# Windowed attention and a gated MLP in one kernel: another order of the opening, and the last score groups in quarters of the array

## The chip, the core and the metric

The kernel runs on one core of a Trainium2 chip. A core has a tensor engine (PE in the profile, with its weight loads as PEld), a vector engine (DVE), a scalar engine (ACT), a general engine (POOL), a queue engine that mostly issues transfers (SP), and 16 DMA engines. Each engine works off its own list of instructions in order and waits on semaphores for the others. The metric is the device time of one execution in microseconds (us); lower is better.

## What is computed

Two blocks follow each other, for a batch of 4, 8 heads, 768 positions, head width 64:

```python
scores = scale * q @ k.T                       # per batch and head
keep   = (pos_k < 4) | ((pos_q - pos_k >= 0) & (pos_q - pos_k < 128))
a      = softmax(where(keep, scores, -1e9))
x      = (a @ v), the 8 heads side by side     # 4 x 768 x 512
h      = gelu_tanh(x @ w_in)                   # 4 x 768 x 1024
u, g   = h[..., :512], h[..., 512:]
g      = layer_norm(g) * g_ln
g      = w_sg @ g + b_sg                       # over the 768 positions
out    = x + (u * g) @ w_out
```

So each query sees four sink positions and the 128 positions up to its own.

## The kernel before

**Pairs.** Two heads make a pair, numbered `n` = 0 to 15; four pairs are one batch element. For a pair, `load` brings k, q and v from memory, 384 KB each (SP's queue; the first q goes through ACT's). k and q come in rows of 1,536 bytes, v in rows of 256 bytes. The pool `loads` holds three of each kind, so the k of pair 3 can start only when the k of pair 0 has been cast. `cast` turns them to bf16, on POOL but for the first two, which go to DVE. `columns` turns k or q by six 128x128 transposes on PE into a PSUM bank (`kps`, `qps`), and one copy by ACT or DVE puts the result into `kT` or `qT` in another element order.

**Scores.** A pair's six blocks of 128 keys are taken in three groups, `g` = 0, 1, 2, of two blocks j each. `score(n, g)` multiplies each block's keys (64 rows of the array per head, so the two heads stand in the upper and lower half) with the 256 queries that can see them (128 for the last block), into a two-bank tile `sc`; there are two such tiles (`ps_s`). In group 2 the free places take the scores of the first 32 keys for the last four query blocks, by eight matmuls that each use 64 rows and 32 columns of the array (line 273). ACT then takes the exponential of the whole tile (line 277).

**The mask.** Positions outside the band are removed in one of two ways. Where `darkened(n, g)` is true, `begin_scores` first writes a large negative number to them by two matmuls of the identity with `off` or `off0` (line 247), and the scores are accumulated on top. Else `keep_band` clears them after the exponential: on DVE by one multiplication with a 0/1 mask (line 286) or on POOL by two selects (lines 294, 296).

**Values.** `values(n, c)` does half of a pair, c = 0 or 1: 10 or 12 small matmuls of probabilities with v and two with the sinks' v (`vsink`), a reciprocal and a multiplication on DVE (lines 328, 329). `turn_x` transposes a pair's result by six PE transposes and one copy. The PSUM pool `ps_m` has four banks, for all of `kps`, `qps`, `av`, `xps` and the MLP's tiles.

**The MLP.** With a batch element's four `xT` there, `open_v` and `hidden` run x @ w_in (tiles `hv`, `hu`), the norm, and later `spatial` (`vs`, line 423) and `project` (`o_ps`, line 454); these fill the time of the next four pairs' attention.

**Order.** The schedule is written out by hand (`manual_schedule`): every engine does its instructions in the order in which the code emits them. Lines 596 to 678 are the opening, the stretch in question: four pairs of attention with nothing to fill the gaps, and the first loads. Before it PE runs 16 small matmuls on the identity (`WARM`) and, after the first transposes, `keep_busy(3)`. SP's queue takes k, q of pair 1, v of pair 0, k, q of pair 2, k of pair 3, four small copies that spread the sinks (`spread_sinks`), q of pair 3, v of pairs 1, 2, 3, and then `hold_loads(0)`, a tiny transfer that waits for the first half of w_in. POOL issues the weight transfers between its casts. `vsink` is cleared in two parts, 13 of 16 pairs' worth by DVE and the rest by POOL (`NZ`).

Of the kernel before, what the change touches and what calls it, by code (L numbers as in the profile page):

```python
# [18 lines left out]
def kernel(  # L19
# [14 lines left out]
    nc = tc.nc  # L34
    V, G, A = nc.vector, nc.gpsimd, nc.scalar
# [7 lines left out]
    NT = S // 128  # L43
    HP = H // 2
    KD = DM // 128
    KU = DF // 128
    NP = B * HP
    HT = NT // 2
# [19 lines left out]
    iden = consts.tile([128, 128], BF16, name="iden")  # L68
# [21 lines left out]
    def load(n, which, eng=None, in_rows=False):  # L90
        b, hp = divmod(n, HP)
        src = dict(k=k, q=q, v=v)[which]
        dst = loads.tile([128, 2, NT, 64], F32, name=which + "_sb")
        order = "h (t p) d -> p h t d" if which == "v" or in_rows else "h (p t) d -> p h t d"
        (eng or nc.sync).dma_start(  # L95
            out=dst, in_=src[b, 2 * hp:2 * hp + 2].rearrange(order, t=NT))
        raw[n, which] = dst
# [3 lines left out]
    def cast(n, which, eng):  # L101
        src = raw.pop((n, which))
        if which == "v":
            eng.tensor_copy(v_bufs[n % NV][:, :, :, 0:64], src)  # L104
            return
        dst = work.tile([128, NT, 128], BF16, name=which + "_bf")
        eng.tensor_copy(dst.rearrange("p t (h d) -> p h t d", h=2), src)  # L107
        flat[n, which] = dst
# [15 lines left out]
    load(0, "k")  # L124
    load(0, "q", A)
    A.dma_start(out=g_rows, in_=moe_g_ln.rearrange("(c p) -> c p", p=128))
    for n, which in ((1, "k"), (1, "q"), (0, "v"), (2, "k"), (2, "q")):
        load(n, which)
    NZ = 13


    DARK = -2.0 ** 33
# [25 lines left out]
    G.memset(off0[0:n_sink, 0:256], 0.0)  # L158
    G.memset(vsink_flat[:, NZ * 520:].bitcast(F32), 0.0)
    V.memset(vsink_flat[:, 0:NZ * 520], 0.0)  # L160
    iden4 = consts.tile([KU, KU], F32, name="iden4")
    V.tensor_copy(iden4, iden[0:KU, 0:KU])

    def band_mask(m, dark):
        V.tensor_scalar(out=m, in0=dark, scalar1=-1.0 / DARK, scalar2=1.0,
                        op0=ALU.mult, op1=ALU.add)

    def spread_sinks(i):

        pairs = slice(0, HP) if i == 0 else slice(HP, NP)  # L170
        for a in range(4):
            nc.sync.dma_start(out=vsink[32 * a:32 * a + n_sink, a, pairs], in_=vst[i])
# [8 lines left out]
    def load_w_in(cols, cs=slice(0, KD)):  # L181
        G.dma_start(out=w_in_sb[:, cs, cols],
                    in_=moe_w_in.rearrange("(c p) f -> p c f", p=128)[:, cs, cols])
# [25 lines left out]
    def bank(shape, dtype, name):  # L209
        return ps_m.tile(shape, dtype, name=name, tag="m")  # L210
# [1 line left out]
    kTs, qTs, exps, avs = {}, {}, {}, {}  # L212
    x_sb, xT = {}, {}

    def columns(n, which, eng):
        src = flat.pop((n, which))
        ps = bank([128, NT, 128], BF16, which + "ps")
        for t in range(NT):
            nc.tensor.transpose(ps[:, t, :], src[:, t, :], iden)  # L219
        dst = work.tile([128, S], BF16, name=which + "T")  # L220
        o, i = dst.rearrange("c (p t) -> c p t", t=NT), ps.rearrange("c t p -> c p t")
        if eng is A:
            A.copy(o, i)
        else:
            eng.tensor_copy(o, i)  # L225
        (kTs if which == "k" else qTs)[n] = dst

    def columns_by_dma(n):
# [6 lines left out]

    def darkened(n, g):

        return (n, g) in ((0, 1), (0, 2), (1, 2), (2, 1), (2, 2), (3, 0), (3, 1), (3, 2), (HP, 0))

    scores = {}  # L240

    def begin_scores(n, g):
        sc = scores[n, g] = ps_s.tile([128, 1024], F32, name="sc", tag="s")
        if darkened(n, g):
            used = 512 if g < HT - 1 else 384
            for l in range(2):
                nc.tensor.matmul(sc[:, 512 * l:512 * l + used], iden,  # L247
                                 (off0 if g == 0 else off)[:, 0:used],
                                 start=True, stop=False)

    def score(n, *groups):
        kT, qT = kTs[n], qTs[n]
        if 0 in groups:
            exps[n] = work.tile([128, HT, 1024], BF16, name="ex", bufs=3)
        for g in groups:
            if (n, g) not in scores:
                begin_scores(n, g)
            sc = scores.pop((n, g))
            w, dark = 0, darkened(n, g)
            for j in (2 * g, 2 * g + 1):  # L260
                n_q = min(256, S - 128 * j)
                for l in range(2):
                    rows = slice(64 * l, 64 * l + 64)
                    nc.tensor.matmul(sc[:, 512 * l + w:512 * l + w + n_q],  # L264
                                     kT[rows, 128 * j:128 * (j + 1)],
                                     qT[rows, 128 * j:128 * j + n_q], start=not dark,
                                     stop=not dark or j % 2 == 1)
                w += n_q
            if g == HT - 1:
                for a in range(4):  # L270
                    for l in range(2):
                        rows = slice(64 * l, 64 * l + 64)
                        nc.tensor.matmul(
                            sc[32 * a:32 * (a + 1), 512 * l + w:512 * (l + 1)], kT[rows, 0:32],
                            qT[rows, 128 * (a + 2):128 * (a + 3)], start=True, stop=True,
                            tile_position=(64 * l, 32 * a))
            A.activation(out=exps[n][:, g, :], in_=sc, func=AF.Exp, scale=scale)  # L277

    def keep_band(n, g, eng):
        if darkened(n, g):  # L280
            return
        ex = exps[n][:, g, :].rearrange("p (l c) -> p l c", l=2)
        w = 512 if g < HT - 1 else 384
        if eng is V:
            m = mask0 if g == 0 else mask
            V.tensor_mul(ex[:, :, 0:w], ex[:, :, 0:w],  # L286
                         m[:, 0:w].unsqueeze(1).to_broadcast([128, 2, w]))
            return
        half = ex[:, :, 0:512].rearrange("p l (j s c) -> p l j s c", j=2, s=2)
        diag, prev = half[:, :, :, 0, :], half[:, :, :, 1, :]  # L290
        if g == HT - 1:
            prev = prev[:, :, 0:1, :]
        nj = prev.shape[2]
        eng.affine_select(out=diag, in_=diag, compare_op=ALU.is_ge, fill=0.0, base=0,  # L294
                          pattern=[[0, 2], [0, 2], [1, 128]], channel_multiplier=-1)
        eng.affine_select(out=prev, in_=prev, compare_op=ALU.is_ge, fill=0.0, base=-1,
                          pattern=[[0, 2], [0, nj], [-1, 128]], channel_multiplier=1)
# [35 lines left out]
    def turn_x(n, eng):  # L333
        b, hp = divmod(n, HP)
        ps = bank([128, NT, 128], BF16, "xps")
        for t in range(NT):
            nc.tensor.transpose(ps[:, t, :], x_sb[b][:, hp, t, :], iden)  # L337
        if eng is A:
            A.copy(xT[b][:, hp, :], ps.rearrange("p t c -> p (t c)"))
        else:  # L340
            eng.tensor_copy(xT[b][:, hp, :], ps.rearrange("p t c -> p (t c)"))
# [248 lines left out]
    def keep_busy(count):  # L590

        ps = bank([128, 512], F32, "idle")
        for i in range(count):
            nc.tensor.matmul(ps, iden, off, start=True, stop=True)

    cast(0, "k", V)
    cast(0, "q", V)
    band_mask(mask, off)
    begin_scores(0, 1)
    columns(0, "k", A)  # L600
    columns(0, "q", V)
    band_mask(mask0, off0)
    keep_busy(3)
    cast(1, "k", G)
    cast(1, "q", G)
    load(3, "k")
    spread_sinks(0)
    load(3, "q")
    load(1, "v")
    load(2, "v")  # L610
    load(3, "v")


    score(0, 0, 1)
    columns(1, "k", V)
    columns(1, "q", V)
    cast(0, "v", G)
    keep_band(0, 0, V)
    cast(2, "k", G)
    cast(2, "q", G)  # L620
    score(0, 2)
    score(1, 0, 1)
    columns(2, "k", A)
    columns(2, "q", V)
    keep_band(1, 0, V)
    cast(3, "k", G)
    cast(3, "q", G)
    score(1, 2)
    for cs in (slice(0, 2), slice(2, KD)):
        load_w_in(slice(DF, d_ff), cs)  # L630
    cast(1, "v", G)
    keep_band(1, 1, G)
    values(0, 0)
    values(0, 1)
    score(2, 0)
    columns(3, "k", A)
    score(2, 1)
    columns(3, "q", V)
    keep_band(2, 0, V)
    cast(2, "v", G)  # L640
    score(2, 2)
    turn_x(0, V)
    values(1, 0)
    score(3, 0)
    values(1, 1)
    score(3, 1)
    values(2, 0)
    score(3, 2)
    cast(3, "v", G)
    load_w_in(slice(0, DF))  # L650
    load_sinks(1)
    load_w_sg()
    values(2, 1)
    turn_x(1, A)

    hold_loads(0, w_in_sb[0:1, 0, DF:DF + 16].bitcast(F32))
# [145 lines left out]
```

## Time and profile before

| | |
|---|---|
| median of 3 runs | 167.34 us (166.82 to 167.85) |
| profiled execution, its own time | 167.47 us |
| its span in the trace | 165.8 us |
| mean granted PE clock | 0.995 |
| PE busy | 154.7 us, 93% of the span |
| DVE, ACT, POOL busy | 132.0, 110.2, 78.0 us |
| DMA | 31.09 MB, 188 GB/s over the span |
| start of the first `hv` matmul, where the opening ends | 24.43 us |
| the chain of work that ended last | PE 80%, DVE 7%, DMA 4% |

The span is 1.7 us shorter than the device time of the same execution; that rest lies around the program's own instructions. The timeline merges neighbouring instructions of one line into a row: start, length, engine, line, operation, output and inputs, shape, count, and in brackets the idle time before the row and what ended it. Matmul lengths contain a modelled run-out of some 0.17 us that overlaps the next one, so the pace of PE is read from start to start.

### The profile page before, as it was taken

To read this page: it belongs to the slowest core of one execution; us is meant where nothing else is said; L and a number is where in the kernel's file an instruction comes from. 1 tells how busy PE (TensorE), PEld (TensorE's weight loads), DVE (VectorE), ACT (ScalarE), POOL (GpSimd) and SP (SyncE) were. 2 spreads that over 40 slices of the span, in tenths; PEclk is the share of its full clock that TensorE was granted. 3 is DMA by queue.
4 is the path that set the end of the run, shared out by engine and by line. 5 is a ranking of instruction groups with operands and counts; after the bars stand their busy time and mean duration, and the time that the engine had idled before them with its cause. 6 is when DMAs were issued, how large, how long until landed. Compare 5 with 4: busy or idle time off the path is not lost.

```text
span 165.8 us, 4053 instructions
## 1 busy us (share of the span) xinstructions
PE 154.7 (93%) x1558; PEld 91.0 (55%) x1558; DVE 132.0 (80%) x316; ACT 110.2 (66%) x150; POOL 78.0 (47%) x115
## 2 busy tenths in 40 slices
PE   3878999999999999999999999999999999999950
PEld 3545574566567665565666645554565645555430
DVE  6776984996899986799889994999999959997520
ACT  3188878879977689598887475679749357511220
POOL 6469771105899979500279997000996000000000
PEclk9999999999999999999999999999999999999997
DMA  4999979999999979999912999899932310040352
GB/s 135 332 324 266 211 91 287 211 305 310 293 228 313 254 250 333 304 213 218 192 66 51 115 239 216 182 237 218 209 65 47 129 65 0 0 183 18 123 198 73
DMA packets 60194, 31.09 MB, mean 188 GB/s; under 512 B 48356, under 2 KB 57080, under 8 KB 60168
## 3 DMA queue, kind: packets, MB, share of 16 engines
q1 hardware_dynamic: 56800, 27.47, 69.4%
q0 software_dynamic: 2944, 2.77, 10.4%
q10 hardware_dynamic: 424, 0.53, 1.0%
q8 instruction: 14, 0.23, 0.6%
q14 instruction: 12, 0.10, 0.2%
HBM read 24.81 MB, written 6.29 MB: 188 GB/s over the span
## 4 chain that ended last, share of the span: by engine, by line
PE 80%; DVE 7%; DMA 4%; SPq 3%; issue 1%; ACT 1%; POOL 1%; POOLq 0%; ACTq 0%
PE vs L423 16%; PE hu L380 13%; PE o_ps L454 11%; PE hv L361 9%; PE av L320 7%; PE sc L264 6%; DMA q_sb<-in_q_dram 4%; PE hv L368 4%; SPq L95 3%; PE xps L337 2%; PE av L326 2%; PE qps L219 2%; PE kps L219 2%; PE o_ps L460 2%; PE sc L247 2%; DVE gv L426 1%
## 5 line engine op out<-in xcount | busy, mean ns | idle before, releaser
L277 ACT ACTIVATE ex<-sc 128x1024 bf16<-128x1024 f32 x48 | 47.5, 1024 | 12.5 <-PE sc L264 9.1
L423 PE MATMUL vs<-wsgT,vn 128*128 128x384 bf16 x192 | 35.3, 326 | 0.1
L294 POOL TENSOR_SCALAR_AFFINE_SELECT ex<-ex 128x512 bf16<-128x512 bf16 x25 | 17.0, 680 | 30.8 <-issue 15.2
L423 PEld LDWEIGHTS <-vn 128*128 128x128 bf16 x192 | 17.7, 97 | 10.5 <-DVE vn L413 0.2
L454 PE MATMUL o_ps<-w_out_sb,gT 128*128 128x512 bf16 x92 | 23.3, 380 | 0.1
L380 PE MATMUL hu<-xT,w_in_sb 128*128 128x384 bf16 x128 | 22.1, 326 | 0.0
L426 DVE SCALAR_TENSOR_TENSOR gv<-vs,g_sb,b_bc 128x384 bf16<-128x384 f32 x32 | 19.5, 611 | 2.7 <-PE vs L423 2.3
L372 DVE BATCH_NORM_STATS2 st<-v_all 128x6 f32<-128x512 f32 x24 | 16.1, 671 | 4.5 <-ACT v_all L370 4.5
L370 ACT ACTIVATE v_all<-hv 128x512 f32<-128x512 f32 x24 | 13.3, 599 | 8.6 <-PE hv L368 8.2
L107 POOL CAST k_bf<-k_sb 128x768 bf16<-128x768 f32 x15 | 12.6, 841 | 13.3 <-DMA k_sb<-in_k_dram 13.2
L361 PE MATMUL hv<-w_in_sb,xT 128*128 128x512 bf16 x72 | 18.8, 379 | 0.0
L329 DVE TENSOR_TENSOR x<-av,rcps 128x384 bf16<-128x384 f32 x32 | 17.8, 557 | 1.1
L429 DVE TENSOR_TENSOR gT<-gv,uT 128x384 bf16<-128x384 bf16 x32 | 17.0, 532 | 1.9
L383 ACT ACTIVATE uT<-hu 128x384 bf16<-128x384 f32 x32 | 15.7, 492 | 4.1 <-PE hu L380 3.7
L463 ACT COPY o_sb<-o_ps 128x512 f32<-128x512 f32 x13 | 7.4, 593 | 14.7 <-PE o_ps L460 13.1
L264 PE MATMUL sc<-qT,kT 64*128 64x256 bf16 x192 | 15.7, 264 | 1.3 <-DVE qT L225 1.1
L380 PEld LDWEIGHTS <-w_in_sb 128*128 128x128 bf16 x128 | 12.3, 98 | 8.0
L320 PE MATMUL av<-v_sb,ex 128*128 128x65 bf16 x352 | 16.1, 195 | 0.0
L104 POOL CAST v_sb<-v_sb 128x768 bf16<-128x768 f32 x16 | 14.6, 912 | 2.4 <-DMA v_sb<-in_v_dram 2.4
L320 PEld LDWEIGHTS <-ex 128*128 128x128 bf16 x352 | 13.0, 98 | 4.2 <-issue 1.1
L107 POOL CAST q_bf<-q_sb 128x768 bf16<-128x768 f32 x15 | 14.1, 940 | 2.4 <-DMA q_sb<-in_q_dram 2.2
L286 DVE TENSOR_TENSOR ex<-ex,mask 128x1024 bf16<-128x1024 bf16 x14 | 13.1, 933 | 2.3 <-ACT ex L277 2.1
(90 smaller groups left out, 219.9 us busy)
## 6 DMA issues: line engine op xcount, KB each, us to landing
k_sb<-in_k_dram SPq DMA_DIRECT2D x16, 384.0 KB, 6.2
v_sb<-in_v_dram SPq DMA_DIRECT2D x16, 384.0 KB, 6.4
out_dram<-o_sb SPq DMA_DIRECT2D x23, 256.0 KB, 2.8
q_sb<-in_q_dram SPq DMA_DIRECT2D x15, 384.0 KB, 6.1
wsg_sb<-in_moe_w_sg_dram POOLq DMA_DIRECT2D x2, 576.0 KB, 11.1
w_in_sb<-in_moe_w_in_dram POOLq DMA_DIRECT2D x2, 256.0 KB, 6.3
w_in_sb<-in_moe_w_in_dram POOLq DMA_DIRECT2D x1, 512.0 KB, 5.5
w_out_sb<-in_moe_w_out_dram POOLq DMA_DIRECT2D x1, 512.0 KB, 8.3
```

The lines of the kernel that those rows point to most:

```text
L107: eng.tensor_copy(dst.rearrange("p t (h d) -> p h t d", h=2), src)
L264: nc.tensor.matmul(sc[:, 512 * l + w:512 * l + w + n_q], kT[rows, 128 * j:128 * (j + 1)], qT[rows, 128 * j:128 * j + n_q], start=not dark, ...
L277: A.activation(out=exps[n][:, g, :], in_=sc, func=AF.Exp, scale=scale)
L294: eng.affine_select(out=diag, in_=diag, compare_op=ALU.is_ge, fill=0.0, base=0, pattern=[[0, 2], [0, 2], [1, 128]], channel_multiplier=-1)
L320: nc.tensor.matmul(av[:, m, l, :], probs(j, l, half), v_sb[:, l, j, :], start=first, stop=False)
L329: V.tensor_mul(x_sb[b][:, hp, HT * c:HT * (c + 1), :].rearrange("p i (l d) -> p i l d", l=2), av[:, :, :, 0:64], rcp.to_broadcast([128, HT ...
L361: nc.tensor.matmul(hvs[b, j], xT[b][:, c, 128 * j:128 * (j + 1)], w_in_sb[:, c, DF:], start=(c == 0), stop=False)
L380: nc.tensor.matmul(h_ps[:, 0:NH], w_in_sb[:, c, 128 * f:128 * (f + 1)], xT[b][:, c, NH * n:NH * (n + 1)], start=(c == 0), stop=(c == KD - 1))
L423: nc.tensor.matmul(vs[:, 0:NH], vns[b][:, si, 128 * f:128 * (f + 1)], wsgT[:, si, cols], start=(si == 0), stop=(si == NT - 1))
L426: V.scalar_tensor_tensor(out=gv, in0=vs[:, 0:NH], scalar=g_sb[:, f:f + 1], in1=b_bc[:, cols], op0=ALU.mult, op1=ALU.add)
L429: V.tensor_mul(gTs[b][:, f, cols], gv, uTs[b][:, f, cols])
L454: nc.tensor.matmul(o_ps, gTs[b][:, c, rows], w_out_sb[:, c, :], start=(c == 0), stop=(c == KU - 1 and not by_act))
```

## The change

It does six things. (1) k and q of all four opening pairs are queued ahead of any v; the sinks' copies follow v of pair 1. (2) `columns` can copy in parts, and the k and q of pair 0 and the q of pair 1 are copied in two halves. (3) Pairs 0 and 1 are wholly masked on PE (groups (0,0), (1,0), (1,1) added), and (2,1) and (3,0) are masked by DVE instead; POOL's selects of (1,1) go. (4) The emission order of the opening is new: the scores and copies of pairs 0 to 2 come before the first `values`, and the k copies of pairs 2 and 3 move from ACT to DVE. (5) DVE clears 10 pairs' worth of `vsink` and POOL 6; the copy to `iden4` comes later; `keep_busy` does 2. (6) In group 2 of every pair the two blocks' scores are made by 16 matmuls of 64 rows and 32 columns in place of 4 of 64 rows and 128 columns.

```diff
--- before.py
+++ after.py
@@ -124,9 +124,10 @@
     load(0, "k")
     load(0, "q", A)
     A.dma_start(out=g_rows, in_=moe_g_ln.rearrange("(c p) -> c p", p=128))
-    for n, which in ((1, "k"), (1, "q"), (0, "v"), (2, "k"), (2, "q")):
-        load(n, which)
-    NZ = 13
+    for n in (1, 2):
+        load(n, "k")
+        load(n, "q")
+    NZ = 10
 
 
     DARK = -2.0 ** 33
@@ -159,7 +160,6 @@
     G.memset(vsink_flat[:, NZ * 520:].bitcast(F32), 0.0)
     V.memset(vsink_flat[:, 0:NZ * 520], 0.0)
     iden4 = consts.tile([KU, KU], F32, name="iden4")
-    V.tensor_copy(iden4, iden[0:KU, 0:KU])
 
     def band_mask(m, dark):
         V.tensor_scalar(out=m, in0=dark, scalar1=-1.0 / DARK, scalar2=1.0,
@@ -212,17 +212,20 @@
     kTs, qTs, exps, avs = {}, {}, {}, {}
     x_sb, xT = {}, {}
 
-    def columns(n, which, eng):
+    def columns(n, which, eng, parts=1):
         src = flat.pop((n, which))
         ps = bank([128, NT, 128], BF16, which + "ps")
         for t in range(NT):
             nc.tensor.transpose(ps[:, t, :], src[:, t, :], iden)
         dst = work.tile([128, S], BF16, name=which + "T")
-        o, i = dst.rearrange("c (p t) -> c p t", t=NT), ps.rearrange("c t p -> c p t")
-        if eng is A:
-            A.copy(o, i)
-        else:
-            eng.tensor_copy(o, i)
+        for h in range(parts):
+            p = slice(128 // parts * h, 128 // parts * (h + 1))
+            o = dst.rearrange("c (p t) -> c p t", t=NT)[:, p, :]
+            i = ps.rearrange("c t p -> c p t")[:, p, :]
+            if eng is A:
+                A.copy(o, i)
+            else:
+                eng.tensor_copy(o, i)
         (kTs if which == "k" else qTs)[n] = dst
 
     def columns_by_dma(n):
@@ -235,7 +238,7 @@
 
     def darkened(n, g):
 
-        return (n, g) in ((0, 1), (0, 2), (1, 2), (2, 1), (2, 2), (3, 0), (3, 1), (3, 2), (HP, 0))
+        return n < 2 or (n, g) in ((2, 2), (3, 1), (3, 2), (HP, 0))
 
     scores = {}
 
@@ -259,12 +262,16 @@
             w, dark = 0, darkened(n, g)
             for j in (2 * g, 2 * g + 1):
                 n_q = min(256, S - 128 * j)
-                for l in range(2):
-                    rows = slice(64 * l, 64 * l + 64)
-                    nc.tensor.matmul(sc[:, 512 * l + w:512 * l + w + n_q],
-                                     kT[rows, 128 * j:128 * (j + 1)],
-                                     qT[rows, 128 * j:128 * j + n_q], start=not dark,
-                                     stop=not dark or j % 2 == 1)
+                for a in range(4 if g == HT - 1 else 1):
+
+                    wide = 32 if g == HT - 1 else 128
+                    for l in range(2):
+                        rows, part = slice(64 * l, 64 * l + 64), slice(wide * a, wide * (a + 1))
+                        nc.tensor.matmul(sc[part, 512 * l + w:512 * l + w + n_q],
+                                         kT[rows, 128 * j + wide * a:128 * j + wide * (a + 1)],
+                                         qT[rows, 128 * j:128 * j + n_q], start=not dark,
+                                         stop=not dark or j % 2 == 1,
+                                         **(dict(tile_position=(64 * l, 32 * a)) if wide == 32 else {}))
                 w += n_q
             if g == HT - 1:
                 for a in range(4):
@@ -596,61 +603,63 @@
     cast(0, "k", V)
     cast(0, "q", V)
     band_mask(mask, off)
+    begin_scores(0, 0)
     begin_scores(0, 1)
-    columns(0, "k", A)
-    columns(0, "q", V)
+    columns(0, "k", A, 2)
+    columns(0, "q", V, 2)
     band_mask(mask0, off0)
-    keep_busy(3)
+    V.tensor_copy(iden4, iden[0:KU, 0:KU])
+    keep_busy(2)
     cast(1, "k", G)
     cast(1, "q", G)
     load(3, "k")
+    load(3, "q")
+    for n in range(2):
+        load(n, "v")
     spread_sinks(0)
-    load(3, "q")
-    load(1, "v")
-    load(2, "v")
-    load(3, "v")
+    for n in range(2, HP):
+        load(n, "v")
 
 
     score(0, 0, 1)
     columns(1, "k", V)
-    columns(1, "q", V)
-    cast(0, "v", G)
-    keep_band(0, 0, V)
     cast(2, "k", G)
     cast(2, "q", G)
     score(0, 2)
-    score(1, 0, 1)
-    columns(2, "k", A)
-    columns(2, "q", V)
-    keep_band(1, 0, V)
+    columns(1, "q", V, 2)
     cast(3, "k", G)
     cast(3, "q", G)
+    score(1, 0, 1)
+    columns(2, "k", V)
+    columns(2, "q", V)
     score(1, 2)
+    score(2, 0)
+    columns(3, "k", V)
+    columns(3, "q", V)
+    score(2, 1)
+    cast(0, "v", G)
     for cs in (slice(0, 2), slice(2, KD)):
         load_w_in(slice(DF, d_ff), cs)
     cast(1, "v", G)
-    keep_band(1, 1, G)
+    keep_band(2, 0, V)
+    score(2, 2)
     values(0, 0)
     values(0, 1)
-    score(2, 0)
-    columns(3, "k", A)
-    score(2, 1)
-    columns(3, "q", V)
-    keep_band(2, 0, V)
+    score(3, 0)
+    keep_band(2, 1, V)
+    turn_x(0, V)
     cast(2, "v", G)
-    score(2, 2)
-    turn_x(0, V)
     values(1, 0)
-    score(3, 0)
+    score(3, 1)
     values(1, 1)
-    score(3, 1)
+    keep_band(3, 0, V)
+    score(3, 2)
     values(2, 0)
-    score(3, 2)
+    values(2, 1)
     cast(3, "v", G)
     load_w_in(slice(0, DF))
     load_sinks(1)
     load_w_sg()
-    values(2, 1)
     turn_x(1, A)
 
     hold_loads(0, w_in_sb[0:1, 0, DF:DF + 16].bitcast(F32))
```

## Prediction

> **What bounds the kernel now.** I read the page first: the engines' busy shares, the strip over time, and the shares of the chain that ended last.
>
> ```profile
> PE 154.7 (93%) x1558; PEld 91.0 (55%) x1558; DVE 132.0 (80%) x316; ACT 110.2 (66%) x150; POOL 78.0 (47%) x115
> ...
> PE   3878999999999999999999999999999999999950
> ...
> PE 80%; DVE 7%; DMA 4%; SPq 3%; issue 1%; ACT 1%; POOL 1%; POOLq 0%; ACTq 0%
> ```
>
> PE is full from the fourth slice (12 us) to the end, so what counts is when PE's list gets through. The busy share hides pace, so next comes PE's timeline, read from start to start.
>
> ```profile
> 8.21 0.61 PE L264 MATMUL sc<-qT,kT 64*128 64x256 bf16 x8 [0.38 <-DVE qT L225]
> 8.75 0.51 PE L219 MATMUL kps<-iden,k_bf 128*128 128x128 bf16 x6
> ...
> 10.13 0.34 PE L264 MATMUL sc<-qT,kT 64*128 64x256 bf16 x4
> 10.40 0.25 PE L273 MATMUL sc<-qT,kT 64*32 64x128 bf16 x8
> 11.18 0.39 PE L264 MATMUL sc<-qT,kT 64*128 64x256 bf16 x4 [0.53 <-DVE qT L225]
> 11.79 0.40 PE L264 MATMUL sc<-qT,kT 64*128 64x256 bf16 x4 [0.22 <-ACT ex L277]
> ...
> 13.08 0.51 PE L219 MATMUL qps<-iden,q_bf 128*128 128x128 bf16 x6 [0.45 <-POOL q_bf L107]
> ...
> 14.12 0.25 PE L273 MATMUL sc<-qT,kT 64*32 64x128 bf16 x8
> 14.30 0.48 PE L320 MATMUL av<-v_sb,ex 128*128 128x65 bf16 x10
> ...
> 24.43 1.47 PE L361 MATMUL hv<-w_in_sb,xT 128*128 128x512 bf16 x6
> ```
>
> From the first score (8.21) to the first `hv` (24.43) the view names 1.2 us of idle PE (0.53, 0.22, 0.45). The opening is nearly all PE work. DVE's timeline shows its own load there:
>
> ```profile
> 7.20 0.96 DVE L225 COPY qT<-qps 128x768 bf16<-128x768 bf16 x1 [0.89 <-PE qps L219]
> ...
> 15.54 0.18 DVE L328 RECIPROCAL rcps<-av 128x6 f32<-128x6 f32 x1
> ...
> 16.23 0.18 DVE L328 RECIPROCAL rcps<-av 128x6 f32<-128x6 f32 x1
> ...
> 18.25 1.53 DVE L286 TENSOR_TENSOR ex<-ex,mask 128x1024 bf16<-128x1024 bf16 x1
> ```
>
> A copy of 768 elements takes 0.96 us, half a pair's values 0.69 (15.54 to 16.23), a mask multiplication 0.69 to 1.53 (the group's shortest and longest).
>
> **The quarters (part 6).** Four score matmuls of 256 columns take 0.33 us when the array's shape changes after them (15.31 to 15.64 in the same view), eight take 0.54 (8.21 to 8.75): four cost 0.21, the change of shape about 0.12. The eight quarter matmuls of line 273 take 0.18 (14.12 to 14.30). Less one change, 0.06 is left, the time of one 128-column stream (six transposes take 0.35), so eight ran side by side. A group 2 now takes 0.27 + 0.18 = 0.45. New: all 24 matmuls have one shape, so one change falls away: streams of 256, 128 and 128 columns, 0.107 + 0.053 + 0.053, start spacing 0.03, one change 0.12, together 0.31 to 0.36. I take 0.36: 0.09 saved per group, 1.4 us over 16, if PE sets the end everywhere. Lower end nothing. Four groups lie in the opening; the other twelve give at most 1.08. DVE is nearly as full as PE there:
>
> ```profile
> 50.00:60.00 10.00, 10.00 (x150) 6.84 (x149) 9.68 (x20) 7.67 (x9) 9.29 (x14) 1.00 0.99 256
> ```
>
> (third number in us: PE, then PEld, DVE 9.68, ACT, POOL). So I count 0.9 of the 1.08.
>
> **The start (parts 2, 3, 5).** The masks of (0,0) are two more 512-column matmuls ahead of the first transposes. At that time two take 1.06 us, 0.43 each without the run-out. PE ends masks at 4.50 + 4 x 0.43 = 6.2 instead of 5.4; the k was ready at 5.70, so the transposes start 0.55 later. Halves win it back: the first score needs only half of qT, 0.54 us instead of 0.96 (384 elements cost 0.56 in line 329's row; bounds 0.48 and 0.56). First score at 8.2: nothing gained. The shorter clearing on DVE (2.88 to 2.2 us) is hidden, since the first cast waits for its k until 5.08; POOL's longer one ends near 5.9, and its next k comes at 6.48; without that cover it would cost 0.7. `iden4` (0.24) falls where DVE waits for pair 1's k; one `keep_busy` less shortens a wait only.
>
> **The loads (part 1).** POOL's casts show the landings: q or k follow each other by 1.06 to 1.1 us, a v takes 1.75. Without v, k2, q2, k3, q3 land at about 9.2, 10.2, 11.3, 12.4 and v of pair 0 at 14.1. On SP, v of pair 3 now waits for the cast of pair 0's v (to 14.9, before 10.6); behind it stand `hold_loads` and pair 4's loads, which waited for w_in until 21.07 anyway. POOL issues w_in after that cast, at 15 as now. v of pair 3 lands near 20.5; its matmuls come at 24. All hidden; uncovered, a late v 3 would cost up to 1 us.
>
> **The new order (part 4), the term that decides.** Exponentials go at 0.98 us each, and there are two `sc` tiles. (0,2) can start at 9.7 as now. Its group ends at 10.5, q of pair 1 is transposed to 11.0, its first half copied to 11.55: score (1,0) at 11.6 (now 11.18). Masks (0.52) and scores (0.33) of (1,0), (1,1) bring PE to 12.75. Then pair 2 is transposed, and DVE copies k and q one after the other, 13.3 to 15.1 (now ACT takes k beside it). PE has finished (1,2) at 14.1 and waits for q until 15.15: 1.0 us. Pair 3 is transposed from 15.5, DVE copies until 17.85. Only now DVE comes to the work that it had begun at 11 before: mask (2,0), values (0,0), (0,1). With 1.2 us for the mask (between 0.69 and 1.53; POOL casts beside it, as beside the 1.53) pair 0 is done at 17.85 + 1.2 + 2 x 0.69 = 20.4. PE arrives at `turn_x(0)` at 18.7 and waits 1.7 us. After that PE needs: rest of the transposes 0.17, values 0.38 + 0.54 + 0.38 + 0.54 + 0.41 + 0.54, score (3,1) 0.85, (3,2) 0.78, two `turn_x` 0.66: 5.25, to 25.7. DVE needs: masks 1.2 and 0.9 (the last with less of POOL beside it), xT 0.47, four values 2.76: 25.7, then `turn_x(2)` 0.33: 26.0. I take 25.8 for the first `hv`: 1.4 later than 24.43 (the four quarter groups are in it).
>
> Bounds: masks at 0.69 give 25.2 (+0.75); at 1.53 DVE reaches 27.05, `hv` 27.4 (+2.9). If PE waits no more than now, only its work counts: -0.4. Masks moved between pairs are even on PE in the sum (two groups of 0.52 added after 8.2, two taken away).
>
> **Sum.** 167.47 (this execution; span 165.8 and 1.67 around it) + 1.4 - 0.9 = 167.97. The median is 0.13 lower: 167.8.
>
> **Rivals.**
> (A) The opening flows as now: DVE's late backlog is bridged, and PE waits 1.2 us as before. For it: k and q come 1 to 2 us earlier, and DVE's work is nearly the same in sum. Against: two copies in a row stand before score (2,0), and three masks and eight values after 17.85. Then -0.4 - 1.08: 165.9; with 0.4 from the halves 165.5. 0.20.
> (B) Slower: PE can't feed 24 pairs of weight load and matmul in 0.36 us. Eight go at once (10.40), but in the values each pair costs 30 ns (12 from 14.68 to 15.05), a row that the array's own 65 columns explain. If the pairs of group 2 go at 30 ns, a group takes 0.72 + 0.12, 0.39 more than now, and this decides in all 16: +6 in all, 174. It decides from about 15 ns a pair (0.45 a group). 0.07.
> The Trainium skill, "TensorE: Matmul & The Clock Gate", section "Wait — 56ns, not 53.3ns?", speaks for (B): matmuls start no closer than about 25 ns apart, however few columns they have. By that a group would last 0.6 us and the sum be about 4 us higher; the eight of line 273 in 0.18 us disagree with it for a burst of eight, and no run here shows one of 24.
> (C) Slower: the masks on DVE last 1.53 us each, beside POOL's casts and weight issues: +2.9 - 0.9, 169.3. 0.12.
> (D) The quarters shorten PE but DVE or ACT set the pace later: +1.4, 168.7. 0.06.
>
> **Chances and range.** The forecast, an opening 0.7 to 2.2 later and quarters worth 0.5 to 1.1, holds 0.55, all within 1% (1.7 us, about what a measurement of this kernel can tell from no change). Faster by over 1%: the better part of (A), 0.12. Slower: (B) and (C), 0.19. Within: 0.69. The range from 165.8 to 169.5 leaves out (B), the best end of (A) and the worst of (C).
>
> **What would show it.** Right: the first score near 8.2; PE idle about 1 us before score (2,0), released by DVE's qT, and 1.5 us at `turn_x(0)`, released by DVE's x; first `hv` near 25.8; the distance from there to the end of PE's list 0.9 shorter than before; rows of 16 and 8 quarter matmuls that begin 0.16 to 0.18 apart, the next row 0.18 on. Wrong: `hv` before 24.5, or the quarter rows further apart than 0.27.

## The result, and the profile after

Run side by side, the changed kernel takes 1.0076 times the time of the kernel before (95% interval 1.0054 to 1.0099). That is some 1.3 us more where 0.5 was forecast, and within the bound of 1% that the prediction called "within". Ten of its 24 runs, and eight of the twelve of after_again and opening_only below, which have the same loads, took 172 us or more and are left out of the ratios, as is one of the 54 runs of the five kernels with v_early's loads. The other fourteen have a median of 168.79 us; the median of all 24 is 169.44, beside 167.36 for the kernel before.

The profiled execution took 173.93 us (span 172.2). Its granted clock (the share of PE's full clock that the profile records) is 1.00 until 50.24 us and 0.5 from there to 57.07, so its page is shown for its form, and its timeline is compared with the kernel before only up to 44 us.

The page of the changed kernel: busy times, PE's strip over 40 slices, and the chain's shares.

```profile
PE 156.8 (91%) x1751; PEld 92.2 (54%) x1751; DVE 136.5 (79%) x320; ACT 109.1 (63%) x149; POOL 76.9 (45%) x113
...
PE   3897899999949999999999999999999999999960
...
PE 61%; DVE 18%; DMA 11%; issue 2%; ACT 2%; POOL 1%; SPq 1%; ACTq 0%; DVEq 0%
```

In the strip the opening's dip, a 7 and an 8, stood in the third and fourth slices (8.3 to 16.6 us) before and stands in the fourth and fifth now (12.9 to 21.5): PE's waits have moved to a later place. The 4 further on (47.4 to 51.7 us) and the larger share of DVE in the chain come from what happened in this execution after 44 us; the last section shows it.

PE's timeline of the changed kernel (start, length, then the group, and in brackets the idle time before it and what ended it):

```profile
8.07 0.86 PE L270 MATMUL sc<-qT,kT 64*128 64x256 bf16 x8 [0.35 <-DVE qT L228]
...
11.50 0.39 PE L270 MATMUL sc<-qT,kT 64*128 64x256 bf16 x4 [0.22 <-DVE qT L228]
...
13.79 0.36 PE L270 MATMUL sc<-qT,kT 64*32 64x256 bf16 x16
13.96 0.24 PE L280 MATMUL sc<-qT,kT 64*32 64x128 bf16 x8
...
15.18 0.39 PE L270 MATMUL sc<-qT,kT 64*128 64x256 bf16 x4 [0.98 <-DVE qT L228]
...
19.23 0.34 PE L344 MATMUL xps<-iden,x 128*128 128x128 bf16 x3 [0.37 <-DVE x L336]
19.92 0.34 PE L344 MATMUL xps<-iden,x 128*128 128x128 bf16 x3 [0.35 <-DVE x L336]
...
24.24 0.47 PE L327 MATMUL av<-v_sb,ex 128*128 128x65 bf16 x10 [0.19 <-POOL v_sb L104]
...
25.48 1.47 PE L368 MATMUL hv<-w_in_sb,xT 128*128 128x512 bf16 x6
```

PE waits 0.98 us for the second of two copies before score (2,0) at 15.18, and 0.37 and 0.35 us for DVE's values at `turn_x(0)`. The first `hv` starts at 25.48, 1.05 later than before. DVE's timeline shows why the waits are where they are:

```profile
16.05 0.96 DVE L228 COPY kT<-kps 128x768 bf16<-128x768 bf16 x1 [0.93 <-PE kps L219]
16.93 0.95 DVE L228 COPY qT<-qps 128x768 bf16<-128x768 bf16 x1
17.79 0.68 DVE L293 TENSOR_TENSOR ex<-ex,mask 128x1024 bf16<-128x1024 bf16 x1
```

The copies of pair 3 stand ahead of the first mask and of every `values`, so DVE begins these at 17.79.

### The profile page after: what moved, and what is told of

It reads as the page before. It is cut to its first block, busy times and chain, and to the rows that moved or that the text cites. A ratio compares the mean times of both kernels' runs of the same rounds, so it can differ in the third digit from the quotient of the medians.

```text
span 172.2 us, 4443 instructions
## 1 busy us (share of the span) xinstructions
PE 156.8 (91%) x1751; PEld 92.2 (54%) x1751; DVE 136.5 (79%) x320; ACT 109.1 (63%) x149; POOL 76.9 (45%) x113
## 4 chain that ended last, share of the span: by engine, by line
PE 61%; DVE 18%; DMA 11%; issue 2%; ACT 2%; POOL 1%; SPq 1%; ACTq 0%; DVEq 0%
PE vs L430 12%; PE hu L387 12%; PE o_ps L461 9%; PE hv L368 9%; DMA v_sb<-in_v_dram 8%; DVE gT L436 5%; DVE gv L433 4%; PE hv L375 3%; PE sc L270 3%; DVE ex L293 3%; PE av L327 3%; DVE x L336 3%; DMA k_sb<-in_k_dram 2%; PE xps L344 2%; ACT ex L284 2%
## 5 line engine op out<-in xcount | busy, mean ns | idle before, releaser
L430 PE MATMUL vs<-wsgT,vn 128*128 128x384 bf16 x192 | 37.2, 338 | 2.1 <-DVE x L336 2.0
L430 PEld LDWEIGHTS <-vn 128*128 128x128 bf16 x192 | 18.2, 100 | 13.6 <-DVE x L336 2.2
L461 PE MATMUL o_ps<-w_out_sb,gT 128*128 128x512 bf16 x92 | 23.3, 379 | 0.5 <-DVE x L336 0.5
L436 DVE TENSOR_TENSOR gT<-gv,uT 128x384 bf16<-128x384 bf16 x32 | 20.1, 627 | 1.9
L379 DVE BATCH_NORM_STATS2 st<-v_all 128x6 f32<-128x512 f32 x24 | 16.1, 671 | 4.5 <-ACT v_all L377 4.5
L270 PE MATMUL sc<-qT,kT 64*128 64x256 bf16 (+2 forms) x384 | 16.5, 258 | 1.9 <-DVE qT L228 1.8
L104 POOL CAST v_sb<-v_sb 128x768 bf16<-128x768 f32 x16 | 13.8, 860 | 8.0 <-DMA v_sb<-in_v_dram 8.0
L470 ACT COPY o_sb<-o_ps 128x512 f32<-128x512 f32 x13 | 7.4, 593 | 14.9 <-PE o_ps L467 13.3
L293 DVE TENSOR_TENSOR ex<-ex,mask 128x1024 bf16<-128x1024 bf16 x14 | 12.1, 863 | 3.7 <-ACT ex L284 3.7
L303 POOL TENSOR_SCALAR_AFFINE_SELECT ex<-ex 128x512 bf16<-128x512 bf16 (+1 forms) x24 | 14.2, 591 | 0.0
```

What stands on the lines that cost most here:

```text
L270: nc.tensor.matmul(sc[part, 512 * l + w:512 * l + w + n_q], kT[rows, 128 * j + wide * a:128 * j + wide * (a + 1)], qT[rows, 128 * j:128 * ...
L293: V.tensor_mul(ex[:, :, 0:w], ex[:, :, 0:w], m[:, 0:w].unsqueeze(1).to_broadcast([128, 2, w]))
L430: nc.tensor.matmul(vs[:, 0:NH], vns[b][:, si, 128 * f:128 * (f + 1)], wsgT[:, si, cols], start=(si == 0), stop=(si == NT - 1))
L436: V.tensor_mul(gTs[b][:, f, cols], gv, uTs[b][:, f, cols])
L461: nc.tensor.matmul(o_ps, gTs[b][:, c, rows], w_out_sb[:, c, :], start=(c == 0), stop=(c == KU - 1 and not by_act))
```

## The experiments

The theory was that two things explain the result: the new order makes PE wait for DVE's queue in the opening (+1.05 us), and the quarters shorten PE's list but not the kernel, since DVE and POOL are as full there. Rivals: the loads' new order costs the time, or the quarters themselves do. As the first score starts at a slightly different time in each execution (7.9 to 8.4 us), the column "between" says how far the first `hv` is behind it. The last column is explained below the table.

| kernel | first score | first `hv` | between | `hv` to last matmul | ratio (95%) | at like clock |
|---|---|---|---|---|---|---|
| before | 8.21 | 24.43 | 16.2 | 135.04 | | |
| changed | 8.07 | 25.48 | 17.4 | | 1.0076 (1.0054 to 1.0099) | |
| quarters_only | 8.35 | 24.45 | 16.1 | 134.93 | 0.9984 (0.9958 to 1.001) | 0.999 |
| opening_only | 8.08 | 25.55 | 17.5 | | | |
| v_early | 8.22 | 25.53 | 17.3 | 135.31 | 1.0069 (1.0043 to 1.0095) | 1.008 |
| k_by_act | 8.21 | 24.82 | 16.6 | 135.38 | 1.0024 (0.9994 to 1.0054) | 1.004 |
| turn_later | 8.45 | 25.68 | 17.2 | 135.02 | 1.0001 (0.9968 to 1.0035) | 1.002 |
| flow_both | 8.12 | 24.80 | 16.7 | 135.31 | 1.0004 (0.9976 to 1.0032) | 1.003 |
| flow_wide | 8.43 | 24.70 | 16.3 | 135.48 | 1.0023 (0.9988 to 1.0058) | 1.004 |
| halves_only | 8.39 | 24.64 | 16.2 | 135.06 | 0.997 (0.9937 to 1.0003) | 1.000 |
| halves_quarters | 7.90 | 24.37 | 16.5 | 134.97 | 0.9944 (0.9914 to 0.9975) | 0.996 |

The kernel before ran again beside each batch of experiments, and its runs in the ratios are of two kinds. In 1 of 11, 7 of 29 and 10 of 35 the mean granted clock was 0.978 to 0.981, and these took 168.23 to 169.16 us; in the rest it was 0.988 or more, with medians of 167.31 to 167.47 us. One run of the first kind was profiled, that of bare_before (a variant of the kernel before, below; mean 0.980): its clock is 0.5 from 13.34 to 16.75 us, and its first `hv` comes at 25.73. None of the 70 runs in the ratios of the kernels with the new order has such a clock. So their ratios mix two things, the new order's own time and the kernel before's occasional late opening. "At like clock" is the median of the runs with a mean clock of 0.985 or more, over the same median of the kernel before beside it. Why the new order has no such run is not shown.

**after_again: the changed kernel once more.**

> The changed kernel as it stands, for a second profile. Theory 1 (the opening costs 1.0 us, the quarters give about 1 us back, and what is lost beyond that comes from loads that arrive late): ratio 1.007, first hv near 25.5 us, v of pair 3 landing near 23 us instead of 20. Theory 2 (the quarters give nothing, since DVE and POOL set the pace after the opening): the same ratio, but then the distance from the first hv to PE's last matmul is not shorter than before's 135.0 us even where no load is waited for.

Ratio 1.0092 (1.0049 to 1.0135), from three of its six runs; first `hv` at 25.48 again. The loss and the opening repeat.

**quarters_only: part 6 alone.** The kernel before with

```diff
-                for l in range(2):
+                for a in range(4 if g == HT - 1 else 1):
+                    wide = 32 if g == HT - 1 else 128
+                    for l in range(2):
...
```

> The kernel before with part 6 alone (16 quarter matmuls in each group 2). Theory 1: 0.09 us less PE time in each of 16 groups, 0.9 to 1.4 us in all: 166.0 to 166.5, ratio 0.992 to 0.995; each group's 24 matmuls in 0.36 us from the first to the next row. Theory 2: ratio 0.998 to 1.002, the same 0.36 us per group, and DVE idle time shrinking by what PE gained.

Measured 167.22 against 167.38 us, ratio 0.9984 (0.9958 to 1.001). Group 2 of one pair, first in the kernel before, then with quarters:

```profile
96.96 0.34 PE L264 MATMUL sc<-qT,kT 64*128 64x256 bf16 x4
97.23 0.25 PE L273 MATMUL sc<-qT,kT 64*32 64x128 bf16 x8
97.41 0.54 PE L320 MATMUL av<-v_sb,ex 128*128 128x65 bf16 x12
```

```profile
96.67 0.36 PE L267 MATMUL sc<-qT,kT 64*32 64x256 bf16 x16
96.84 0.24 PE L277 MATMUL sc<-qT,kT 64*32 64x128 bf16 x8
97.02 0.54 PE L324 MATMUL av<-v_sb,ex 128*128 128x65 bf16 x12
```

From the group's start to the next work it was 0.45 us (96.96 to 97.41) and is 0.35 (96.67 to 97.02): the 0.10 is there, in each of 16 groups. Of the 1.2 us that twelve of them make after the opening, 0.11 reaches the end (135.04 to 134.93). The rest became waits. Busy time by engine from 93 to 99 us (PE, PEld, DVE, ACT, POOL), of the kernel before and of quarters_only:

```profile
93.00:99.00 6.00, 5.98 (x70) 3.22 (x67) 5.86 (x12) 3.31 (x4) 6.00 (x10) 1.00 1.07 205
```

```profile
93.00:99.00 6.00, 5.53 (x80) 3.13 (x80) 5.86 (x12) 2.90 (x4) 6.00 (x9) 1.00 1.14 215
```

PE's share falls from 5.98 to 5.53, DVE's stays at 5.86 and POOL's at 6.00 of 6 us: PE was full, but not alone. The view of PE's waits in quarters_only (total, times, longest) says for whom it now waits; none of these three groups is in that view of the kernel before.

```profile
PE o_ps L458 <- DVE x L333: 0.6, 2, 0.4
...
PE kps L219 <- DVE k_bf L107: 0.3, 1, 0.3
PE av L324 <- POOL ex L298: 0.2, 1, 0.2
```

**opening_only: parts 1 to 5 without the quarters.** The changed kernel with the score loop of before.

> The changed kernel with group 2 as before (4 matmuls of 128 columns of the array per group), so parts 1 to 5 alone. Theory 1: first hv near 25.8 us, time 168.6 + 0.9 = 169.5, ratio 1.013. Theory 2: 168.6, ratio 1.007.

Its six runs spread from 170.11 to 177.38 us and give no ratio; its time is inconclusive. Its trace has the first `hv` at 25.55, so the opening is late without the quarters too.

**v_early: the loads near their old places.** The changed kernel with

```diff
-        dst = loads.tile([128, 2, NT, 64], F32, name=which + "_sb")
+        dst = loads.tile([128, 2, NT, 64], F32, name=which + "_sb", bufs=4 if which == "v" else 3)
...
-    for n in range(2):
-        load(n, "v")
     spread_sinks(0)
-    for n in range(2, HP):
+    for n in range(HP):
         load(n, "v")
```

> The changed kernel with the sinks' four small copies ahead of the v loads on SP's queue, and a fourth buffer for raw v, so that v of pairs 2 and 3 wait neither for descriptors behind the sinks nor for the cast of pair 0. Theory 1 (late loads cost what is lost beyond the opening): v of pair 3 lands near 20 us instead of 23.3, the second half of w_in near 27 instead of 30.4, and the time falls by 0.4 to 0.9 us, ratio 0.999 to 1.003. A rival (loads are hidden, the loss is the opening's stalls alone): the loads land as early but the time stays at ratio 1.007.

First the rows that made the loads suspect, of the changed kernel, on SP's queue and on POOL:

```profile
9.74 4.91 SPq L172 DMA_DIRECT2D vsink<-vst  x4
14.70 1.54 SPq L95 DMA_DIRECT2D v_sb<-in_v_dram  x2
```

```profile
20.28 0.87 POOL L104 CAST v_sb<-v_sb 128x768 bf16<-128x768 f32 x1 [3.45 <-DMA v_sb<-in_v_dram]
23.36 0.83 POOL L104 CAST v_sb<-v_sb 128x768 bf16<-128x768 f32 x1 [2.21 <-DMA v_sb<-in_v_dram]
```

The sinks' four small copies took SP 4.91 us to issue behind two loads of v (2.66 before), and v of pair 3 is cast at 23.36 instead of 20.08. In v_early that cast starts at 19.91, and the ratio is 1.0069 (1.0043 to 1.0095), the first `hv` at 25.53: as slow as the changed kernel. So the late loads are real and cost nothing that the ratio shows, and theory 1 of this experiment falls. What came of them after 44 us in the changed kernel's profiled execution is a matter for the last section.

**k_by_act, turn_later, flow_both: the two waits.** v_early with pair 2's k copied by ACT, as before the change; with `turn_x(0)` behind score (3,1); with both.

```diff
-    columns(2, "k", V)
+    columns(2, "k", A)
...
-    turn_x(0, V)
...
     score(3, 1)
+    turn_x(0, V)
```

> v_early with two edits against the two waits of PE in the new opening: pair 2's k is copied by ACT beside DVE's copy of q, and turn_x(0) is emitted after score (3,1) instead of before values (1,0). Theory 3 (the 1.1 us that the change costs is these two waits and DVE's backlog behind them): the wait ahead of score (2,0) falls from 1.0 to about 0.5 us, the one at turn_x(0) goes, first hv near 24.9 instead of 25.5, time 0.5 us below v_early's 168.7, ratio 1.003. If the waits only move to DVE's values: first hv 25.4 and ratio 1.007.

> The v_early kernel with one more edit: pair 2's k is copied by ACT, not DVE. Theory (two waits of PE, one before score (2,0) and one at turn_x(0), both fed by one backlog of copies on DVE): the first wait falls from 0.98 to about 0.4 us as in flow_both, DVE has its copies done 0.95 us earlier, and the second wait shrinks by itself: first hv 24.8 to 25.0, ratio 1.000 to 1.003. Rival (the two waits are separate, and each has its own share): hv 25.1 to 25.3, ratio near 1.004, with 0.7 us or more of PE idle still at turn_x(0).

> The v_early kernel with one more edit: turn_x(0) stands behind score (3,1). Theory (one backlog on DVE): the wait of 0.98 us before score (2,0) stays, the waits at turn_x(0) are filled by score (3,1), but what DVE is late with only moves on to the next wait: hv 25.2 to 25.5, ratio 1.005 to 1.007. Rival (two separate waits): hv falls by the whole wait at turn_x(0), to 24.9 to 25.1, ratio near 1.003.

PE's timeline of flow_both:

```profile
14.66 0.39 PE L270 MATMUL sc<-qT,kT 64*128 64x256 bf16 x4 [0.41 <-ACT kT L226]
...
19.84 0.51 PE L344 MATMUL xps<-iden,x 128*128 128x128 bf16 x6
...
24.80 1.43 PE L368 MATMUL hv<-w_in_sb,xT 128*128 128x512 bf16 x5
```

and of turn_later:

```profile
15.55 0.39 PE L270 MATMUL sc<-qT,kT 64*128 64x256 bf16 x4 [0.98 <-DVE qT L228]
...
20.39 0.51 PE L344 MATMUL xps<-iden,x 128*128 128x128 bf16 x6
...
23.94 0.48 PE L327 MATMUL av<-v_sb,ex 128*128 128x65 bf16 x10 [0.26 <-DVE ex L293]
...
25.68 0.38 PE L368 MATMUL hv<-w_in_sb,xT 128*128 128x512 bf16 x1
```

flow_both has 0.41 us of wait before score (2,0) and none at `turn_x(0)`, and its ratio is 1.0004 (0.9976 to 1.0032). At like clock 0.45 us (167.76 beside 167.31) are left of v_early's loss of 1.33 (168.69 beside 167.36). So the opening's order is where most of the time went. k_by_act alone gives `hv` at 24.82, as the theory of one backlog on DVE said: one copy of 0.95 us taken off DVE shortens both waits (PE's timeline has 0.41 before score (2,0) and 0.35 at `turn_x(0)`). Its ratio, 1.0024, is within what was expected; at like clock 0.62 us are left, so this one copy brings back about half.

For turn_later the trace and the time disagree. The trace does what the theory said: the wait at `turn_x(0)` goes and comes back at 23.94, `hv` stands 17.2 behind the first score instead of 17.3, and DVE runs without a pause from 16.43 to past 25 us. But its time, 167.87 us in the median beside 167.58, is as good as flow_both's, outside what was expected of it; its profiled execution, 168.22 us, is not one of its better ones. Part of its late `hv` is a mask: the one at 20.16 took 1.27 us beside a cast that POOL had begun at 20.06, where all three of k_by_act took 0.68. Whether its other runs had a short mask there is not known, so how much the second edit alone is worth stays open.

**flow_wide: flow_both without the quarters.**

> The flow_both kernel with group 2's scores in 128 columns of the array, as before the change. If the quarters shorten PE's own work and DVE, POOL and ACT take it back, this is as fast as flow_both: ratio 0.999 to 1.003, group 2 at 0.45 us instead of 0.35, first hv 24.9 to 25.2, and from hv to the last matmul 135.0 to 135.3. If the quarters are worth what the forecast counted, 0.9 us, the ratio is 1.005 to 1.007 and hv to the last matmul is 136 or more.

Ratio 1.0023 (0.9988 to 1.0058) against flow_both's 1.0004, at like clock 1.0038 against 1.0027, and 135.48 against 135.31 from `hv` to the last matmul. With the opening mended the quarters are again worth 0.17 us behind it, and some 0.2 to 0.3 us in all; the 0.9 of the forecast is not there, with either opening.

**bare_before and bare_quarters: DVE relieved.** The main loop of the kernel before, and of quarters_only, without this line; the mask of group 0 is left out for pairs 5 to 15.

```diff
-            keep_band(n, 0, V)
```

> The kernel before without DVE's mask multiplications of pairs 5 to 15 (keep_band(n, 0, V) in the main loop left out, so those groups keep their unmasked probabilities); it is the base for bare_quarters. Theory 2 (DVE sets the pace of the attention stretches together with PE): eleven multiplications of 0.69 to 1.2 us go, and some of it shows, 165.5 to 166.9. A rival (PE alone sets the pace): 167.2 to 167.4, unchanged.

> The same omission with the quarter matmuls of part 6 added. Each group 2 lasted 0.45 us before and 0.35 with quarters, so PE has 1.6 us less to do in 16 groups. Theory 2 (DVE took that back): with DVE relieved it shows, 0.7 to 1.4 us below bare_before. A rival (PE's own list, by instruction supply or fixed waits, took it back): within 0.3 us of bare_before.

167.38 us with quarters, 168.44 without; against the kernel before 0.9958 (0.9916 to 1.0) and 1.0027 (0.9987 to 1.0066). The sign is the theory's, but the intervals touch. At like clock the medians are 166.44 and 168.24 us, further apart; but bare_before, which does less than the kernel before, then comes out slower than it (167.31), which no theory here accounts for. Their traces say more. From the first `hv` to that of the second batch element lie four groups 2, which save 0.4 us of PE's work: with DVE relieved the quarters bring all of it (39.79 to 39.39), with the masks 0.17 (39.80 to 39.63). Then, in bare_quarters, the next limit takes it back:

```profile
95.58 0.61 PE L267 MATMUL sc<-qT,kT 64*128 64x256 bf16 x8 [1.30 <-DMA qT<-q_bf]
```

Here q is turned by a DMA transpose, and PE, early, waits 1.30 us for it. The test is inconclusive as a time and in favour of the theory as a trace.

**halves_only and halves_quarters: the parts that cost nothing.** The kernel before with `columns` in parts and

```diff
-    columns(0, "k", A)
-    columns(0, "q", V)
+    columns(0, "k", A, 2)
+    columns(0, "q", V, 2)
```

and the same with the quarters.

> The kernel before with pair 0's k and q copied in halves (part 2 alone). By the prediction's step the first score waits for half of qT: it starts 0.4 us earlier, at 7.8 instead of 8.2, and the gain is then lost in the waits for q of pairs 1 and 2, so ratio 0.998 to 1.000. A rival (the start carries through the opening): first hv 0.4 us earlier, ratio 0.997.

> The kernel before with two parts of the change alone: the k and q of pair 0 copied in two halves, and group 2 in quarters. No new order, no new loads, no more masks on PE. If both parts bring what they brought alone and add up (0.997 and 0.998), the ratio is 0.994 to 0.997, 166.4 to 166.9 us, first score 7.9 to 8.4, first hv 24.0 to 24.5. If both were within the noise, the ratio is 0.998 to 1.001.

Alone the halves give 0.997 (0.9937 to 1.0003), and 1.000 at like clock. The first score of the profiled execution, at 8.39, is no earlier, and the trace says why: PE was not waiting for the copy, but still at the filler of `keep_busy(3)`.

```profile
6.97 1.49 PE L597 MATMUL idle<-off,iden 128*128 128x512 bf16 x3
8.39 0.71 PE L267 MATMUL sc<-qT,kT 64*128 64x256 bf16 x8
```

The filler takes 0.87 us in the kernel before and 1.01 in halves_quarters, where the score came right behind it:

```profile
6.96 1.01 PE L601 MATMUL idle<-off,iden 128*128 128x512 bf16 x3
7.90 0.77 PE L270 MATMUL sc<-qT,kT 64*128 64x256 bf16 x8
```

That is 0.31 us earlier than in the kernel before, and the first `hv` (24.37) is 0.06 earlier: the head start is lost in the opening, as was expected of it. Halves and quarters together: 166.89 us, 0.9944 (0.9914 to 0.9975), at like clock 166.77 beside 167.47 us (0.996). This version is faster than both kernels. Where it gains can't be read off its trace: the profiled execution, 167.34 us, is one of its slower ones.

## Why the prediction was right, and where it was not

The opening was right in its mechanism and nearly in its size. The total lies in the range, but 0.8 us above the forecast, for the gain that was to cancel most of the opening's loss hardly came.

- **The start.** First score forecast at 8.2, measured 8.07. POOL's longer clearing (4.46 to 5.85) was not as well covered as said, since DVE's first cast beside it took 1.20 us instead of 0.56, to 6.26; but PE was at its two added masks until about then, and the first transposes began at 6.32, the 0.6 later that the masks alone were to cost.
- **The wait before score (2,0).** Forecast 1.0 us, to 15.15; measured 0.98, to 15.18. The copies on DVE were to end at 17.85; the mask behind them started at 17.79.
- **The wait at `turn_x(0)`.** Forecast 1.7 us, measured 0.37 + 0.35. The mis-sized term is the mask on DVE: taken at 1.2 us, it took 0.68, the lower bound. It brought pair 0's values 0.5 us earlier than forecast, and PE's rest took 0.3 longer, so `hv` came at 25.48 (+1.05) and not at 25.8 (+1.4), between the forecast and the lower bound of 25.2. Rival (C), masks of 1.53, did not happen in any opening traced here with the new order; 1.35 did, in v_early.
- **The loads.** "All hidden" held for the time, but the step's landings were wrong: v of pair 3 was to land near 20.5 and came at 23.3. Its issue was forecast well (after 14.9, measured 15.3); what was mis-sized is the time from there to its landing, 5.6 us by the forecast, 7.0 in the kernel before and 8.0 now, beside w_in that POOL issues from 14.54. What it costs PE in the opening is the 0.19 at 24.24.
- **The quarters.** The size per group was right (0.09 forecast, 0.10 measured), and rival (B) is refuted: 24 matmuls take 0.35 us and not 0.84. The Trainium skill's page "TensorE: Matmul & The Clock Gate", section "Wait — 56ns, not 53.3ns?", speaks of a least spacing of about 25 ns between matmul starts; these rows, 16 in 0.17 us on quarters of the array, disagree.
- **The step that failed: "I count 0.9 of the 1.08".** PE's gain per group was taken as time, less a little for DVE, though the row shown beside it had DVE at 9.68 of 10 us and POOL at 9.29. Measured, 0.1 to 0.3 arrives. This is the mechanism of rival (D), which was given 0.06 and 168.7 us; the kernel before's median times the ratio is 168.6. That (D)'s number fits so well is in part luck, since its opening was 1.4 and not the measured 1.05. A row with three engines at 93% or more should have had that case as the main one.

So the sum was +1.4 - 0.9 = +0.5. The traces show +1.05 in the opening and, in v_early, +0.27 behind the first `hv` with the quarters' gain already in it (135.04 to 135.31; without the quarters flow_wide has 135.48). What lengthens that part is not traced further; in turn_later it is 135.02.

## What to carry to other kernels

An engine that is full sets the pace alone only if the others in that stretch have room: before a gain on one engine is counted, read the same window for all of them, and expect waits in place of time where two or three are full. In a hand-written order the place where a copy is emitted can matter as much as its length: two copies of 0.95 us put ahead of the first mask and values delayed everything behind them, and giving one of them to another engine brought about half of the loss back. Parts of a change should be timed apart: here two parts together gain 0.4 to 0.6% and the whole loses 0.8%. And before a small ratio is read, compare the granted clock of the runs on both sides: here it moved some by 0.2 to 0.3%.

## What the runs showed of the hardware

A mask multiplication on DVE takes 0.68 us, or up to 1.54 in these openings, by what POOL does when it starts. DVE's row and POOL's of v_early:

```profile
19.93 1.35 DVE L293 TENSOR_TENSOR ex<-ex,mask 128x1024 bf16<-128x1024 bf16 x1
```

```profile
19.91 0.83 POOL L104 CAST v_sb<-v_sb 128x768 bf16<-128x768 f32 x1 [0.60 <-DMA v_sb<-in_v_dram]
```

The cast started 0.02 us earlier and ended at 20.74; the mask ended at 21.28, 0.54 after it. In the kernel before, the mask of 1.53 us that the prediction showed (18.25 to 19.78) stood beside two instructions of POOL:

```profile
17.82 0.65 POOL L296 TENSOR_SCALAR_AFFINE_SELECT ex<-ex 128x512 bf16<-128x512 bf16 x1
18.41 0.83 POOL L104 CAST v_sb<-v_sb 128x768 bf16<-128x768 f32 x1
```

They end at 19.24, and again the mask is done 0.54 later: by these rows the second POOL instruction went ahead of a mask that was already waiting. It is not always so: at 45.62 in the same trace a mask went ahead of the next cast, which then took 1.28 us instead of 0.83. In the opening of the changed kernel no instruction of POOL was under way when a mask started, and all three masks took 0.68. The Trainium skill's page "SBUF — State Buffer", section "Who interferes with whom", says that a DVE instruction with two SBUF inputs contends with a POOL instruction that reads SBUF, and that the one that issues first has the shared ports to its end; the rows agree, and add that a second POOL instruction can pass. The doubled masks of v_early and flow_both (1.28 at 17.27) come and go with the landing of v, so the price of a mask depends on the loads.

More than one can pass. In the profiled execution of the changed kernel a DVE multiplication that took 0.36 us at 42.79 takes 3.35 at 46.07, while POOL goes through four instructions in a row. Rows of DVE, of POOL and of PE:

```profile
46.07 3.35 DVE L436 TENSOR_TENSOR gT<-gv,uT 128x384 bf16<-128x384 bf16 x1
```

```profile
46.48 0.41 POOL L303 TENSOR_SCALAR_AFFINE_SELECT ex<-ex 128x256 bf16<-128x256 bf16 x1
46.86 0.81 POOL L107 CAST k_bf<-k_sb 128x768 bf16<-128x768 f32 x1
47.62 0.82 POOL L107 CAST q_bf<-q_sb 128x768 bf16<-128x768 f32 x1
48.40 0.82 POOL L104 CAST v_sb<-v_sb 128x768 bf16<-128x768 f32 x1
```

```profile
51.22 2.10 PE L430 MATMUL vs<-wsgT,vn 128*128 128x384 bf16 x6 [2.00 <-DVE x L336]
```

PE waits 2.00 us for what stands behind it on DVE, and from 50.24 to 57.07 us the granted clock is 0.5. POOL is late there: its cast of the next k starts at 40.13 us, in v_early at 37.81. after_again and opening_only, with the same late loads, have a DVE instruction of 6.71 and of 3.36 us in the same stretch; in the eleven other traces no multiplication on DVE takes more than 1.54. So the late loads may cost more than the ratio shows; no run was made to test that.
